# Batch 1's attention inside a fused attention and MoE kernel: shared query rows and one burst of transposes

## The chip, the cores and the metric

The kernel runs on one core of one Trainium2 chip. The metric is device time in microseconds of one execution, taken as the median of several runs. In the text, TensorE is the matmul engine (PE in the profile; PEld are its weight loads), VectorE is DVE, ScalarE is ACT, GpSimd is POOL, and SP is the engine whose queue issues the output DMAs.

## The reference

For 8 batches of 8 heads, 576 tokens and 64 channels a head, two attentions are computed and added. One is local: each query sees the keys at a distance under 4. The other is pooled: queries, keys and values are averaged over groups of 4 tokens, 144 queries attend to 144 keys, and each result is repeated for its 4 tokens. The sum, as 4608 rows of 512 channels, goes through a feed-forward layer.

```
out_d = sm_attn(q_d, k_d, v_d)            # means over groups of 4 tokens
out_up = np.repeat(out_d, factor, axis=2)
scores = np.where(mask, scores, -1e9)     # |i - j| < 4
out_local = np.matmul(attn, v)
x = (out_up + out_local) as [B * S, H * D]
h = x @ w_in;  g = h / (1 + exp(-1.702 h));  out = g @ w_out
```

## The kernel before

**Order of the work.** The order on every engine is the order in which the program's text issues instructions; nothing is rescheduled. The feed-forward layer (the MoE matmuls) runs over 9 groups of 512 tokens. For group g, `mm1` (L732) multiplies x by w_in into 16 blocks of 128 hidden channels, 4 matmuls of 128x512 each, and ScalarE applies the sigmoid product to each block (L728). `mm2` (L749) multiplies by w_out, 16 matmuls into each of four token tiles of 128 tokens (L781), and ScalarE evicts each tile (L766) before it is stored. While group g runs, the attention of batch g + 1 is put between these matmuls: `attention` (L666 to L714) returns a list of pieces, and a list of positions says before which step each piece goes. Steps 0 to 15 are the hidden blocks of `mm1`, step 16 + n is matmul n of `mm2`. Group 0 has its own list, `POS_0` (L811), and batch 1 is the batch that it carries. Other batches go by `POS` (L810); batch 0 is written out by hand ahead of the loop.

**PSUM.** There are three double tiles PA[0] to PA[2], each of two banks, and two single ones, PM[0] and PM[1] (in the profile all are pa and pm). The MoE matmuls use PM in turn, and in group 0 also PA[0]: token tiles 0 and 1 accumulate in PM, tiles 2 and 3 in the two banks of PA[0], in the order of eight matmuls at a time, tiles 0 and 1 first and tiles 2 and 3 from matmul 16. Attention's scores take all three double tiles. Batch 1's other pieces use PA[1] and PA[2] only (`slots`, the pair of heads taken modulo 2). Group 1 begins with two blocks at once, one in PM and one in PA[1].

**A batch's attention.** Heads go in pairs (`hp`, 0 to 3), two pairs at a time as far as the scores:

- Scores of two pairs (`scores_mixed`, L365 and L377): 80 matmuls of a 32-row, 64-column tile for five chunks of local keys and 24 for the pooled keys. ScalarE takes the exponentials (L415, L421), and VectorE zeroes what lies outside the band (L429).
- `av` (L446, L468): 20 matmuls with the local weights and 20 with the pooled ones, each a tile of 64 rows and 64 columns, so that four of them lie in the array. A 65th column of ones gives the sums for the softmax. In each matmul the 64 output partitions are queries of one head; the two heads of a pair stand in different halves of the partitions.
- `normalise` (L484, L485): VectorE takes the reciprocals of the sums and multiplies, from PSUM to `y` in bf16.
- `transp` (L499, L509): 26 matmuls with the identity, again tiles of 64 rows and 64 columns, turn `y` into channels by tokens, as fp32 in a double tile. Each handles one head.
- `copy_od` (L623): ScalarE copies the 144 pooled results, each four times, to `od` in SBUF, in two instructions. `od` has two buffers.
- `merge` (L644, L650): VectorE adds the local results and `od` and writes the pair's rows of `xT`, which `mm1` of the next group reads.

Batch 1's pieces and steps before the change: scores of pairs 0 and 1 at 16, their exponentials at 18, the second scores with exponentials at 30, values and normalisation of pairs 0 and 1 at 46, transposes and merge of pair 0 at 52 and of pair 1 at 56, values of pairs 2 and 3 at 65, transposes and merge of pair 2 at 71 and of pair 3 at 75. Step 79 is the last matmul of group 0. At step 41 a further piece computes the pooled values on TensorE (L334).

Of the kernel before, what the change touches and what calls it, by code (L numbers as in the profile page):

```python
# [8 lines left out]
FP32 = mybir.dt.float32  # L9
BF16 = mybir.dt.bfloat16  # L10
AF = mybir.ActivationFunctionType
ALU = mybir.AluOpType
# [7 lines left out]
def kernel(  # L20
# [9 lines left out]
    nc = tc.nc  # L30
    B, H, S, D = q.shape
    SD = S // 4
    HP = H // 2
# [16 lines left out]
    work = ctx.enter_context(tc.tile_pool(name="work", bufs=2))  # L50
# [9 lines left out]
    xT = [persist.tile([128, B * S], BF16, name=f"xT{i}") for i in range(HP)]  # L60
    vbs = [persist.tile([128, 5, H, 65], BF16, name=f"vb{i}") for i in range(2)]
    vds = [persist.tile([128, 3, HP, 65], BF16, name=f"vd{i}") for i in range(2)]
    es = [persist.tile([128, 2, 304], BF16, name=f"es{i}") for i in range(4)]
    eds = [persist.tile([128, 2, 480], BF16, name=f"ed{i}") for i in range(2)]
# [7 lines left out]
    def ps_tile(n=None):  # L72
        if n is None:
            n = turn["a"] % 3
            turn["a"] += 1
        return PA[n]

    def pm_tile():
        turn["m"] += 1
        return PM[turn["m"] % 2]  # L80
# [60 lines left out]
    def ident(pos, n, c0, c1):  # L141
        return id128[64 * pos : 64 * pos + n, 64 * pos + c0 : 64 * pos + c1]
# [277 lines left out]
    def exp_down(qd, sd):  # L420
        nc.scalar.activation(  # L421
            out=eds[qd][:, :, 0:432], in_=sd[:, :, 0:432],
            func=AF.Exp, scale=inv_sqrt_d / 16.0,
        )
# [66 lines left out]
    def transp(y, n=None):  # L491
# [23 lines left out]
                )  # L515
        return x

    def av_local0(hp, o, chunks):
        E, vb = es[hp], vbs[0]
        for i in chunks:  # L520
            for j in range(2):
                for par in range(2):
                    pos, c0 = i % 2, 65 * (i // 2 * 2 + j)
                    nc.tensor.matmul(  # L524
                        o[64 * pos : 64 * pos + 64, par, c0 : c0 + 65],
                        lhsT=E[64 * par : 64 * par + 64, j, 60 * i : 60 * i + 64],
                        rhs=vb[64 * par : 64 * par + 64, i, 2 * hp + j, :],
                        start=True, stop=True,
                        tile_position=(64 * par, 64 * pos),
                    )  # L530
# [98 lines left out]
    def sub(t, off, *dims):  # L629
        return bass.AP(  # L630
            tensor=t.tensor, offset=t.offset + off,
            ap=[list(t.ap[0])] + [list(d) for d in dims],
        )
# [22 lines left out]

    def warm(n, cols=512, t=None, z=wz):
        t = pm_tile() if t is None else t  # L660
        for _ in range(n):
            nc.tensor.matmul(
                t[:, 0:cols], lhsT=z[:, 0:128], rhs=z[:, 0:cols], start=True, stop=True
            )

    def attention(b, slots=None):  # L666
        st = {}

        def s_pe(qd):
            st["s", qd], st["d", qd] = scores_mixed(b, qd)  # L670

        def s_act(qd):
            if qd == 0:
                nc.scalar.preload_act_table_set("exp_and_others")
            exp_local(qd, st["s", qd])
            exp_down(qd, st["d", qd])
            if qd == 1:
                nc.scalar.preload_act_table_set("silu_and_others")
            mask_local(qd)

        def s1():
            s_pe(1)
            s_act(1)

        def avn(*hps):
            def f():
                for hp in hps:
                    st["o", hp] = av(b, hp, slots and slots[hp % 2])
                for hp in hps:
                    st["y", hp] = normalise(st["o", hp])  # L690
            return f

        def tr(*hps):
            def f():
                for hp in hps:
                    st["x", hp] = transp(st["y", hp], slots and slots[hp % 2])
                for hp in hps:
                    od = copy_od(st["x", hp])
                    merge(b, hp, st["x", hp], od)
            return f  # L700

        first = [lambda: s_pe(0), lambda: s_act(0), s1, avn(0, 1)]
        if b == 1:
            return first + [tr(0), tr(1), avn(2, 3), tr(2), tr(3)]

        def av_tr():
            for hp in (2, 3):
                st["o", hp] = av(b, hp)
            st["x", 0] = transp(st["y", 0])
            for hp in (2, 3):  # L710
                st["y", hp] = normalise(st["o", hp])
            merge(b, 0, st["x", 0], copy_od(st["x", 0]))

        return first + [av_tr, tr(1, 2, 3)]  # L714

    def hps_mm(g, ffc, dmc, acc):
        nc.tensor.matmul(  # L717
# [90 lines left out]
            f()  # L808

    POS = [13, 16, 35, 45, 56, 69]  # L810
    POS_0 = [16, 18, 30, 46, 52, 56, 65, 71, 75]  # L811
    VDP_0 = 41

    o, y, x = {}, {}, {}
# [89 lines left out]
    for g in range(n_groups):  # L904
        b = g + 1
# [33 lines left out]
        if b < B:  # L939
            for n, f in zip(POS if g else POS_0, attention(b, None if g else (1, 2))):  # L940
                steps.setdefault(n, []).append(f)
# [37 lines left out]
```

## Time and profile before

| | before |
|---|---|
| runs, us | 320.72, 318.91, 321.6; median 320.72 |
| profiled execution, us | 320.13 |
| its span, us | 318.4 |
| mean granted TensorE clock | 0.995 |
| TensorE busy, matmuls | 301.9 us, 95% |
| ScalarE, GpSimd, VectorE busy | 58%, 44%, 41% |
| DMA | 40.02 MB, mean 126 GB/s |

The profile shows one execution. The span runs from the first instruction to the last; the profiled execution's own time is 1.7 us more. A group's row names line, engine, operation, what is written and read, and how often; a row of a timeline gives start, length, and in brackets how long the engine stood idle before and what ended that. The chain of waits follows the execution back from its last instruction, at each step to what released it. "issue" is time in which an engine waited for nothing that the profile shows. Matmuls overlap in the array: a MoE matmul's row is 379 ns long, but the next one starts 216 ns behind it. Some matmul records can be missing from a trace.

### The profile page before, as it was taken

The numbers are of one execution on the slowest core, as the hardware profiler recorded it, in microseconds if no ns is written. First come the engines' busy times: TensorE is split into PE (matmuls) and PEld (weight loads), VectorE is DVE, ScalarE is ACT, GpSimd is POOL, SyncE is SP. The second block draws the span as 40 slices with busy tenths as digits, with TensorE's granted clock in tenths as the row PEclk, the third lists the DMA queues.
The fourth block names the chain that finished last, engine by engine and source line by source line (L and its number), as shares of the span: only waits on it lengthen the run. The fifth ranks groups of instructions, "written<-read, shape, count | busy, mean of one in ns | idle before, by whom it ended". The sixth has DMA issues, their size and how long they took to land.

```text
span 318.4 us, 10941 instructions
## 1 busy us (share of the span) xinstructions
PE 301.9 (95%) x4872; PEld 156.5 (49%) x4923; DVE 130.3 (41%) x219; ACT 184.9 (58%) x320; POOL 138.7 (44%) x170
## 2 busy tenths in 40 slices
PE   7699999999899999999999999999999999999995
PEld 4465454545454555445545454445445544444444
DVE  5855625831575047704780288017811650000000
ACT  5445782567546684659465846584667556415611
POOL 8773790099227940695059604980294000000000
PEclk9979999999999999999999999999999999999999
DMA  7999999999949923995299619961810210020011
GB/s 120 118 200 209 182 126 213 166 229 227 165 128 203 207 64 103 190 209 101 72 197 205 128 48 213 206 136 39 176 41 3 70 68 2 0 99 33 2 65 67
DMA packets 64078, 40.02 MB, mean 126 GB/s; under 512 B 44064, under 2 KB 55456, under 8 KB 64032
## 3 DMA queue, kind: packets, MB, share of 16 engines
q1 hardware_dynamic: 44496, 24.32, 37.3%
q0 software_dynamic: 19392, 14.95, 33.8%
q8 instruction: 38, 0.62, 0.9%
q14 instruction: 8, 0.07, 0.1%
q10 hardware_dynamic: 144, 0.07, 0.1%
HBM read 44.83 MB, written 9.44 MB: 170 GB/s over the span
## 4 chain that ended last, share of the span: by engine, by line
PE 91%; issue 3%; DMA 2%; DVE 1%; POOL 1%; ACT 1%; POOLq 0%
PE pm L781 35%; PE pm L717 35%; PE pa L717 4%; PE pa L365 2%; PE pa L377 2%; DMA qb<-in_q_dram 2%; PE pa L781 2%; PE pa L446 2%; PE pa L499 2%; PE pa L468 2%; PE pm L796 1%; PE pm L334 1%; PE pa L509 0%; PE pa L524 0%; DVE qT L267 0%
## 5 line engine op out<-in xcount | busy, mean ns | idle before, releaser
L717 PE MATMUL pm<-xT,w_in_bf 128*128 128x512 bf16 x495 | 118.2, 379 | 1.2 <-ACT xT L616 0.2
L781 PE MATMUL pm<-w_out_bf,gT 128*128 128x512 bf16 x499 | 114.4, 379 | 4.2 <-issue 4.1
L728 ACT ACTIVATE gT<-pm 128x512 bf16<-128x512 f32 x128 | 76.3, 598 | 43.7 <-PE pm L717 43.7
L717 PEld LDWEIGHTS <-w_in_bf 128*128 128x128 bf16 x576 | 55.7, 98 | 66.5 <-issue 0.5
L781 PEld LDWEIGHTS <-gT 128*128 128x128 bf16 x560 | 52.1, 98 | 60.1 <-issue 0.8
L429 DVE TENSOR_TENSOR es<-es,mask 128x600 bf16<-128x600 bf16 x28 | 17.6, 643 | 94.6 <-ACT es L415 93.8
L297 POOL TENSOR_TENSOR pq<-kT 128x576 f32<-128x576 bf16 x13 | 15.1, 1165 | 70.5 <-DVE kT L267 70.5
L766 ACT ACTIVATE osb<-pm 128x512 f32<-128x512 f32 (+2 forms) x35 | 20.5, 586 | 38.2 <-PE pm L781 30.3
L623 ACT COPY od<-pa 128x384 f32<-128x384 f32 (+1 forms) x56 | 19.0, 407 | 27.2 <-PE pa L509 20.7
L485 DVE TENSOR_TENSOR y<-pa,rc 128x896 bf16<-128x896 f32 x28 | 30.6, 1092 | 1.0
L415 ACT ACTIVATE es<-pa 128x600 bf16<-128x600 f32 x32 | 19.7, 668 | 9.5 <-PE pa L365 9.4
L644 DVE TENSOR_TENSOR xT<-pa,od 128x570 bf16<-128x570 f32 x28 | 21.0, 752 | 8.8 <-ACT od L623 8.8
L313 POOL TENSOR_TENSOR v<-v 112x512 f32<-112x512 f32 x18 | 23.0, 1279 | 0.0
L768 DVE TENSOR_SCALAR osb<-pm 128x128 f32<-128x128 f32 x1 | 0.3, 291 | 55.0 <-ACT osb L766 55.0
L267 DVE STREAM_TRANSPOSE kT<-kb 128x576 f32<-128x576 f32 x16 | 20.0, 1250 | 4.3 <-DMA kb<-in_k_dram 4.2
L267 DVE STREAM_TRANSPOSE qT<-qb 128x576 f32<-128x576 f32 x16 | 19.9, 1242 | 0.6 <-POOL kdT L301 0.2
L717 PE MATMUL pa<-xT,w_in_bf 128*128 128x512 bf16 x64 | 20.0, 379 | 0.0
L307 POOL CAST vb<-vf 128x2560 bf16<-128x2560 f32 x6 | 13.9, 2319 | 13.7 <-DMA vf<-in_v_dram 11.3
L365 PEld LDWEIGHTS <-kT 32*64 32x64 bf16 x1280 | 14.2, 104 | 7.7 <-issue 4.9
L365 PE MATMUL pa<-qT,kT 32*64 32x60 bf16 x1280 | 16.4, 198 | 1.3 <-DVE qT L267 1.3
L221 POOL DMA_DIRECT2D vb<-in_v_dram x20 | 13.7, 698 | 9.1 <-DMA w_in_bf<-in_moe_w_in_dram 4.0
L297 POOL TENSOR_TENSOR pq<-qT 128x576 f32<-128x576 bf16 x14 | 16.0, 1145 | 0.1
(90 smaller groups left out, 274.2 us busy)
## 6 DMA issues: line engine op xcount, KB each, us to landing
out_dram<-osb SPq DMA_DIRECT2D x35, 256.0 KB, 2.1
vf<-in_v_dram SPq DMA_DIRECT2D x60, 128.0 KB, 6.8
v<-in_v_dram SPq DMA_DIRECT2D x36, 192.0 KB, 5.5
kb<-in_k_dram POOLq DMA_DIRECT2D x16, 288.0 KB, 7.2
qb<-in_q_dram POOLq DMA_DIRECT2D x16, 288.0 KB, 8.6
w_in_bf<-in_moe_w_in_dram POOLq DMA_DIRECT2D x4, 512.0 KB, 7.2
w_out_bf<-in_moe_w_out_dram POOLq DMA_DIRECT2D x4, 512.0 KB, 12.9
vb<-in_v_dram POOLq DMA_DIRECT2D x20, 64.0 KB, 6.4
```

The lines of the kernel that those rows point to most:

```text
L267: nc.vector.transpose(out=t32.rearrange("p (i c) -> p c i", c=18), in_=store[b, qd].bitcast(FP32).rearrange("p (c d) -> p c d", c=18),)
L297: nc.gpsimd.tensor_tensor(out=t1, in0=sv[:, :, 0:2, :], in1=sv[:, :, 2:4, :], op=ALU.add)
L313: eng.tensor_tensor(out=t1[0:112], in0=x[:, :, 0:2, :], in1=x[:, :, 2:4, :], op=ALU.add)
L365: nc.tensor.matmul(sp[r // 2][64 * par : 64 * par + 64, r % 2, 60 * i : 60 * i + 60], lhsT=kT[b, qd][rows, k0 : k0 + 64, a], rhs=qT[b, qd] ...
L415: nc.scalar.activation(out=es[2 * qd + u][:, :, 0:300], in_=sp[u][:, :, 0:300], func=AF.Exp, scale=inv_sqrt_d,)
L485: nc.vector.tensor_tensor(out=y[:, xs], in0=ov[:, :, :, 0:D], in1=rc[:, xs].to_broadcast([128, n, 7, D]), op=ALU.mult,)
L623: nc.scalar.copy(out=od[:, 4 * t0 : 4 * (t0 + n)].rearrange("p (t f) -> p t f", f=4), in_=x[:, xx, 288 : 288 + n, None].to_broadcast([128, ...
L644: eng.tensor_tensor(out=sub(xT[hp], t0 + 3, (57, 2), (114, 5), (1, 57)), in0=sub(x, 3, (509, 2), (57, 5), (1, 57)), in1=sub(od, 3, (57, 2) ...
L717: nc.tensor.matmul(acc, lhsT=w_in_bf[:, dmc, ffc * 128 : (ffc + 1) * 128], rhs=xT[dmc][:, g * TG : g * TG + TG], start=(dmc == 0), stop=(d ...
L728: nc.scalar.activation(out=gT[:, ffc, :], in_=acc, func=AF.Silu, scale=GELU_SCALE)
L766: eng.activation(out=osb, in_=ap, func=AF.Copy, scale=1.0 / GELU_SCALE)
L781: nc.tensor.matmul(ops[t], lhsT=gT[:, ffc, t * 128 : (t + 1) * 128], rhs=w_out_bf[:, ffc, :], start=(ffc == 0), stop=(ffc == n_ffc - 1),)
```

## The change

Only batch 1's attention is changed, and of that the pieces behind the scores, and the list of steps.

- `av_rows` puts both heads of a pair on the same partitions. A matmul is still a tile of 64 by 64, and there are still 40 for a pair, in another order: chunk i of the queries goes to the lower or upper 64 partitions by i's parity, and the heads stand beside each other in columns.
- `normalise_rows` has the same two VectorE instructions, and then a copy of 64x64 on ScalarE that brings one head's block beside the other's.
- `transp_rows` takes 60 or 64 rows and both heads' 128 columns at once: 13 matmuls for a pair instead of 26, tiles of 64 rows and 128 columns, in transpose mode, with bf16 output. The outputs of two pairs share a double tile (`x_pair`: 0 and 2 in PA[1], 1 and 3 in PA[2]).
- `copy_od_rows` copies the pooled results four times each, as 256 and 320 columns; `merge_rows` adds in three instructions, of 456, 117 and 3 columns.
- The pieces are now: scores at 16, exponentials at 18, second scores at 29, values of pairs 0 and 1 at 46, values of pairs 2 and 3 at 54, and at 65 the transposes of all four pairs in one burst, followed by their copies and merges.

```diff
@@ -515,6 +515,78 @@
                 )
         return x
 
+    def av_rows(b, hp, n=None):
+        o = ps_tile(n)
+        E, Ed, vb, vd, u = es[hp], eds[hp // 2], vbs[b % 2], vds[b % 2], hp % 2
+
+        def local(i, par, j):
+            pos, c0 = i % 2, 65 * (i // 2 * 2 + j + par)
+            nc.tensor.matmul(
+                o[64 * pos : 64 * pos + 64, par, c0 : c0 + 65],
+                lhsT=E[64 * par : 64 * par + 64, j, 60 * i : 60 * i + 64],
+                rhs=vb[64 * par : 64 * par + 64, i, 2 * hp + j, :],
+                start=True, stop=True,
+                tile_position=(64 * par, 64 * pos),
+            )
+
+        def down(kc, j, pos, slot, q0, last=2):
+            nc.tensor.matmul(
+                o[64 * pos : 64 * pos + 64, j, 65 * slot : 65 * slot + 65],
+                lhsT=Ed[64 * j : 64 * j + 48, u, SD * kc + q0 : SD * kc + q0 + 64],
+                rhs=vd[64 * j : 64 * j + 48, kc, hp, :],
+                start=(kc == 0), stop=(kc == last),
+                tile_position=(64 * j, 64 * pos),
+            )
+
+        for i in (0, 2):
+            for j in range(2):
+                for par, e in ((0, 0), (1, 1), (1, 0), (0, 1)):
+                    local(i + e, par, j)
+        left = [(local, (4, par, j)) for j in range(2) for par in range(2)]
+        left += [(down, (kc, j, 0, 6 - 6 * j, 0)) for kc in range(3) for j in range(2)]
+        right = [(down, (0, j, 1, 5 + j, 64, 0)) for j in (1, 0)]
+        right += [(down, (kc, j, 1, 6 - 6 * j, 64)) for kc in range(3) for j in (1, 0)]
+        right += [(down, (kc, j, 1, 4 + j, 128)) for kc in range(3) for j in (1, 0)]
+        for n in range(len(right)):
+            for side in (left, right):
+                if n < len(side):
+                    side[n][0](*side[n][1])
+        return o
+
+    def normalise_rows(o):
+        y = work.tile([128, 14, D], BF16, name="y", tag="y", bufs=4)
+        rc = work.tile([128, 2, 7, 1], FP32, name="rc", tag="rc")
+        ov = o[:, :, 0:455].rearrange("p x (c e) -> p x c e", e=65)
+        nc.vector.reciprocal(rc, ov[:, :, :, 64:65])
+        nc.vector.tensor_tensor(
+            out=y.rearrange("p (x c) d -> p x c d", x=2),
+            in0=ov[:, :, :, 0:D], in1=rc.to_broadcast([128, 2, 7, D]), op=ALU.mult,
+        )
+        nc.scalar.copy(out=y[64:128, 5, :], in_=y[64:128, 12, :])
+        return y
+
+    def x_pair(n=None):
+        t = ps_tile(n).rearrange("p x n -> p (x n)").bitcast(BF16)
+        t = t.rearrange("p (x n) -> p x n", x=2)
+        return [t[:, :, 512 * u : 512 * u + 512] for u in range(2)]
+
+    def transp_rows(y, x):
+        def put(pos, c0, n, src):
+            nc.tensor.matmul(
+                x[:, pos, c0 : c0 + n], lhsT=src, rhs=ident(pos, src.shape[0], 0, n),
+                is_transpose=True, start=True, stop=True, tile_position=(64 * pos, 0),
+            )
+
+        for m in range(3):
+            for par in range(2):
+                for pos in range(2 if m < 2 else 1):
+                    c0 = 8 * par + 2 * m
+                    put(pos, 120 * m + 60 * par, 60, y[64 * pos : 64 * pos + 60, c0 : c0 + 2, :])
+                if m == 2:
+                    c0 = 6 - 2 * par
+                    put(1, 240 + 64 * par, 64, y[64:128, c0 : c0 + 2, :])
+        put(0, 360, 64, y[0:64, 6:8, :])
+
     def av_local0(hp, o, chunks):
         E, vb = es[hp], vbs[0]
         for i in chunks:
@@ -656,6 +728,28 @@
 
 
 
+    def copy_od_rows(x):
+        od = work.tile([128, S], FP32, name="od", tag="od")
+        for xx, c0, t0, n in ((0, 360, 0, 64), (1, 240, 64, 80)):
+            nc.scalar.copy(
+                out=od[:, 4 * t0 : 4 * (t0 + n)].rearrange("p (t f) -> p t f", f=4),
+                in_=x[:, xx, c0 : c0 + n, None].to_broadcast([128, n, 4]),
+            )
+        return od
+
+    def merge_rows(b, hp, x, od):
+        t0 = b * S
+        row = x.ap[1][0]
+        for at, col, dims, from_x in (
+            (3, 3, ((228, 2), (114, 2), (1, 114)), ((120, 2), (row, 2), (1, 114))),
+            (459, 243, ((1, 117),), ((1, 117),)),
+            (0, 0, ((1, 3),), ((1, 3),)),
+        ):
+            nc.vector.tensor_tensor(
+                out=sub(xT[hp], t0 + at, *dims), in0=sub(x, col, *from_x),
+                in1=sub(od, at, *dims), op=ALU.add,
+            )
+
     def warm(n, cols=512, t=None, z=wz):
         t = pm_tile() if t is None else t
         for _ in range(n):
@@ -699,9 +793,25 @@
                     merge(b, hp, st["x", hp], od)
             return f
 
-        first = [lambda: s_pe(0), lambda: s_act(0), s1, avn(0, 1)]
-        if b == 1:
-            return first + [tr(0), tr(1), avn(2, 3), tr(2), tr(3)]
+        def avn_rows(*hps):
+            def f():
+                for hp in hps:
+                    st["o", hp] = av_rows(b, hp, slots[hp % 2])
+                for hp in hps:
+                    st["y", hp] = normalise_rows(st["o", hp])
+            return f
+
+        def tr_rows():
+            for u in range(2):
+                st["x", u], st["x", u + 2] = x_pair(slots[u])
+            for hp in range(HP):
+                transp_rows(st["y", hp], st["x", hp])
+            for hp in range(HP):
+                merge_rows(b, hp, st["x", hp], copy_od_rows(st["x", hp]))
+
+        scores_first = [lambda: s_pe(0), lambda: s_act(0), s1]
+        if slots:
+            return scores_first + [avn_rows(0, 1), avn_rows(2, 3), tr_rows]
 
         def av_tr():
             for hp in (2, 3):
@@ -711,7 +821,7 @@
                 st["y", hp] = normalise(st["o", hp])
             merge(b, 0, st["x", 0], copy_od(st["x", 0]))
 
-        return first + [av_tr, tr(1, 2, 3)]
+        return scores_first + [avn(0, 1), av_tr, tr(1, 2, 3)]
 
     def hps_mm(g, ffc, dmc, acc):
         nc.tensor.matmul(
@@ -808,7 +918,7 @@
             f()
 
     POS = [13, 16, 35, 45, 56, 69]
-    POS_0 = [16, 18, 30, 46, 52, 56, 65, 71, 75]
+    POS_0 = [16, 18, 29, 46, 54, 65]
     VDP_0 = 41
 
     o, y, x = {}, {}, {}

```

## The prediction

> **What bounds the kernel now.** I read the page first, then the chain of waits from 40 to 62 us, the stretch in which batch 1's attention lies, then the timelines of TensorE, ScalarE and VectorE there, and last the groups by shape.
>
> ```profile
> PE 301.9 (95%) x4872; PEld 156.5 (49%) x4923; DVE 130.3 (41%) x219; ACT 184.9 (58%) x320; POOL 138.7 (44%) x170
> ...
> q8 instruction: 38, 0.62, 0.9%
> ...
> PE 91%; issue 3%; DMA 2%; DVE 1%; POOL 1%; ACT 1%; POOLq 0%
> ```
>
> TensorE is the bound almost from end to end: 95% busy, 91% of the chain. Whatever shortens its own queue is worth its full time; work on the others costs only where TensorE waits. So I look for the places where TensorE does not start the next matmul in time. Start time, length and piece in the chain:
>
> ```profile
> 44.47 0.66 ACT es L415
> ...
> 45.17 2.10 PE pa L781 x9
> ...
> 51.89 0.37 issue
> 52.27 0.21 PE pa L509 x3
> ...
> 53.78 0.16 issue
> 53.94 1.67 PE pa L781 x7
> 55.61 0.22 PE pm L781
> ...
> 58.05 0.14 issue
> 58.19 0.35 PE pa L499 x20
> ```
>
> Three kinds of holes: at 45.17 a MoE matmul into PA[0] waits for the exponential that reads PA[0]; at 51.89 and 58.05 TensorE stands inside or before a transpose burst with nothing to wait for; and 0.16 us of "issue" follows each burst. The last kind is no wait. The timeline of TensorE, matmuls and then weight loads:
>
> ```profile
> 52.41 1.04 PE L781 MATMUL pm<-w_out_bf,gT 128*128 128x512 bf16 x4
> 53.38 0.35 PE L499 MATMUL pa<-id,y 60*64 60x60 bf16 x20
> 53.56 0.22 PE L509 MATMUL pa<-id,y 48*64 48x48 bf16 x6
> 53.94 1.67 PE L781 MATMUL pa<-w_out_bf,gT 128*128 128x512 bf16 x7 [0.16 <-issue]
> 55.45 0.38 PE L781 MATMUL pm<-w_out_bf,gT 128*128 128x512 bf16 x1
> ...
> 60.91 0.38 PE L717 MATMUL pm<-xT,w_in_bf 128*128 128x512 bf16 x1
> ```
> ```profile
> 53.71 0.55 PEld L781 LDWEIGHTS <-gT 128*128 128x128 bf16 x4
> ```
>
> Between this burst (step 56) and the next (step 65) the program has nine matmuls; the rows show 7 + 1, and the weights of a first one are loaded at 53.71, 0.23 us before the first recorded one. One record is missing and its matmul sits in the "issue". So a transpose burst costs from 53.07 (52.41 plus three steps of 0.216 and a slow first one) to 53.71, less the normal step: 0.64 - 0.22 = 0.42 us. Of that 26 x 8.2 ns = 0.21 is streaming, 0.09 getting in and 0.12 getting out.
>
> ```profile
> 57.24 0.81 PE L781 MATMUL pm<-w_out_bf,gT 128*128 128x512 bf16 x3
> ```
>
> The two real holes are 0.56 us (0.37 idle plus the 0.19 that the last matmul still ran) before 52.27, and 0.21 before 58.19: the third of this row starts at 57.67, and a burst otherwise begins 0.31 behind (53.38 - 53.07). They have one thing in common with the later ones:
>
> ```profile
> 84.51 0.28 PE L468 MATMUL pa<-vd,ed 48*64 48x65 bf16 x9 [0.88 <-issue]
> 88.51 0.21 PE L446 MATMUL pa<-vb,es 64*64 64x65 bf16 x1 [0.19 <-issue]
> 220.57 0.22 PE L499 MATMUL pa<-id,y 60*64 60x57 bf16 x4 [0.17 <-issue]
> ```
>
> Counted in the program's list of TensorE instructions they stand at 1726, 1982, 2750, 3006 and 7870 (one more, 0.32 us, at 7614, time 216.57, too short to show as a row of its own): all 190 past a multiple of 256. The page's instruction queue moved 38 packets, 0.62 MB, for 9,795 recorded instructions: 63 B each, so a packet carries 256. I read these holes as waits for the next block of instructions, where a block is eaten in under some 5 us because it is full of small matmuls. They are 0.56 + 0.21 in batch 1 and 1.07 + 0.38 + 0.32 + 0.36 = 2.1 us later, again with 0.19 added to each row's idle time.
>
> **The change part by part.** The sum is made against the profiled execution, 320.13 us, of which 318.4 is the span; the three runs' median, 320.72, is 0.6 above it.
>
> Second scores at step 29 instead of 30. The chain above: three matmuls instead of two then lie between these scores and the first one into PA[0]. Scores and exponential both move 0.22 us earlier, and the hole at 45.17 shrinks by as much. Scores of pooled keys go into PA[2], which the first pair's exponential still reads:
>
> ```profile
> 42.34 0.90 ACT L421 ACTIVATE ed<-pa 128x864 bf16<-128x864 f32 x1
> ```
> ```profile
> 43.55 0.27 PE L377 MATMUL pa<-qdT,kdT 32*64 32x144 bf16 x4
> ```
>
> It ends at 43.24; they now come at 43.55 - 0.22 = 43.33, so the cover holds by 0.1. **-0.22** (0 if it is missed).
>
> Transposes. Removed: 4 bursts of 26, 4 x 0.42 = 1.70 us. Added: one of 52, each half the array high and all of it wide. No transpose-mode matmul is in this trace; the nearest shape is L547:
>
> ```profile
> 20.66 0.27 PE L547 MATMUL pa<-vd,ed 48*128 48x65 bf16 x6
> ```
> ```profile
> 20.65 0.15 PEld L547 LDWEIGHTS <-ed 48*128 48x128 bf16 x6
> ```
> ```profile
> L547 PE MATMUL pa<-vd,ed 48*128 48x65 bf16 x24 | 1.1, 194 | 0.0
> ...
> L781 PE MATMUL pm<-w_out_bf,gT 128*128 128x512 bf16 x499 | 114.4, 379 | 4.2 <-issue 4.1
> ```
>
> (0.27 - 0.19) / 5 = 16 ns from one to the next, the two halves alternating as in the new code. 52 x 16 = 0.83, with in and out 1.04: **-0.65**. Low end 8.2 ns as now (-1.07); high end no overlap of loads, whose row has 0.15 us for six of some 95 ns, so 52 x 0.095 = 4.9 (+3.5). I take 16, from the row of the same tile shape.
>
> The Trainium skill, TensorE: Matmul & The Clock Gate, section LDWEIGHTS, speaks against this part: a load takes columns / 1.2 ns, whatever its rows, so twice the columns cost what half the loads save. By its 107 ns, two halves side by side, the burst would be an estimated 52 x 53 ns = 2.8 us and the whole change 1.1 us slower than before. L547's row disagrees: 16 ns.
>
> Attention-times-value bursts. 40 matmuls a pair as now, the same columns, four of them left on half the tiles: +0.05. Both bursts go before all transposes, so the second (step 54) needs PA[1] and PA[2] from VectorE:
>
> ```profile
> 49.88 0.24 DVE L484 RECIPROCAL rc<-pa 128x14 f32<-128x14 f32 x1 [3.69 <-PE pa L468]
> 50.16 1.09 DVE L485 TENSOR_TENSOR y<-pa,rc 128x896 bf16<-128x896 f32 x1
> ...
> 51.43 1.09 DVE L485 TENSOR_TENSOR y<-pa,rc 128x896 bf16<-128x896 f32 x1
> 53.25 0.76 DVE L644 TENSOR_TENSOR xT<-pa,od 128x570 bf16<-128x570 f32 x1 [0.73 <-ACT od L623]
> 54.04 0.17 DVE L650 TENSOR_TENSOR xT<-pa,od 128x6 bf16<-128x6 f32 x1
> ```
>
> All moved by 0.22: PA[1] is free at 51.03, PA[2] at 52.30. The first burst is left at 49.90 and eight matmuls (1.73) end at 51.73; PA[2] is wanted at 52.2. Instruction 1726 now falls 21 matmuls into this burst, at 51.9; its block, which came at 52.27, comes then or 0.2 sooner. Together 0.3 us of waiting here, in place of the 0.56 in the transposes. Instruction 1982 now falls seven MoE matmuls behind the transpose burst, at 57.7, some 5.7 us after 1726 where 5.9 were needed (52.27 to 58.19); what is left of its 0.21 goes into the wait at the end of the stretch. **-0.77 + 0.3 = -0.47** (bounds: -0.77 when the block comes in time, +0.6 when both holes stay and another opens). TensorE then stands at 52.85; eleven matmuls (2.37) later, the burst.
>
> Behind the burst. It runs 55.3 to 56.15, and 15 MoE matmuls (3.24) bring TensorE to group 1 at 59.45. Its first matmul overwrites the PSUM tile of token tile 0, whose eviction is now queued on ScalarE behind eight copies of od; with two od buffers, copies 3 and 4 wait for merges 1 and 2.
>
> ```profile
> 53.84 0.70 ACT L623 COPY od<-pa 128x384 f32<-128x384 f32 x2 [0.61 <-PE pa L509]
> 57.44 0.60 ACT L766 ACTIVATE osb<-pm 128x512 f32<-128x512 f32 x1 [2.90 <-PE pm L781]
> ```
>
> Outputs 0 and 2 share PA[1], so the first copy waits for 39 transposes: 56.1. A copy pair keeps its 576 columns, 0.70: 56.8. A merge is now 456 + 117 + 3 columns; with L644's 570 in 0.75 and L650's 6 in 0.17, 1 ns a column and some 0.16 fixed: 0.63 + 0.28 + 0.17, overlapping by 0.08: 0.9, step 0.83. Merges 1 and 2 end 57.75 and 58.6, copy pair 4 runs 58.65 to 59.35, the eviction ends 59.9. Group 1 starts at 59.95, a wait of **+0.45** (0 to +0.9). Merges 3 and 4 end at 59.5 and 60.3, before TensorE wants PA[1] (second matmul, 60.15) and their rows (fifth and seventh, 60.8 and 61.2). The four 64x64 copies on ScalarE, 0.25 each, lie in its idle time (2.90 us before 57.44).
>
> Sum: -0.22 - 0.65 + 0.05 - 0.47 + 0.45 = **-0.85**. No DMA, and nothing on SP's and GpSimd's queues, changes place; TensorE waits for no landing in this stretch now and reaches none more than 0.5 us sooner.
>
> Later batches. 104 instructions fewer shift every later block border against the bursts. Blocks made of bursts and some 20 loads or matmuls of the MoE stay about as many, so I take 0; bounds -2.1 (all later holes close) and +2 (as much opens).
>
> **The rivals.**
> - The block borders fall well: -0.85 - 2.1 gives 317.8. For: the holes hang on position. Against: half of the comparable blocks have no hole now, so little is to be had beyond it.
> - The borders fall badly: +2, 321.9.
> - The chain behind the burst is longer (od buffers, a late merge): from +0.45 to +1.4, 320.8. For: it has no slack, and VectorE and ScalarE alternate in it.
> - Slower: the wide transposes do not overlap their loads as L547 does. At 95 ns, two halves side by side: 52 x 48 ns = 2.5 us instead of 0.83, +1.7, 321.5; one after another: 4.9, +4.1, 324.0. The change breaks even at (0.83 + 0.85) / 52 = 32 ns each. Against it: L547. The page's load rule, above, is the first of the two.
> - Slower: TensorE's clock drops in the burst. It has dropped once:
>
> ```profile
> 16.00:24.00 8.00, 7.72 (x191) 5.30 (x192) 4.64 (x13) 3.83 (x7) 5.97 (x10) 0.79 1.23 200
> ...
> 49.00:61.00 12.00, 10.85 (x297) 5.94 (x300) 8.21 (x15) 3.92 (x11) 0.18 (x1) 1.00 1.08 198
> ```
>
> At 0.79 (the last column but two) the burst and the 15 matmuls behind it, 4.1 us, take 1.1 us more: 321.0; at half speed 4.1 more: 324.0. Now the clock is 1.00 through four bursts. The Trainium skill's page TensorE: Matmul & The Clock Gate, PE-mode transpose, says that such transposes do not count as busy; no run here shows it, and one microsecond is little.
>
> **How the numbers follow.** 320.72 - 0.85 = 319.87, so 319.8 for the likeliest case, with 318.8 to 320.7 as its own range. Chances: forecast 0.58, good borders 0.14, bad borders 0.06, longer chain 0.11, transposes half overlapped 0.04, serial 0.04, clock 0.03. The runs themselves lie 2.7 us apart, and 1%, 3.2 us, is about what a measurement of this kernel can tell from no change. Low end 317.7 takes in the good borders, high end 321.9 the longer chain, the half overlapped transposes and the bad borders; the serial transposes are outside. Faster by over 1% needs good borders and a better batch 1: 0.11. Slower by over 1%: serial transposes, most of the clock, and a bad draw of borders on top of another loss: 0.09. Within 1%: 0.80.
>
> **What would show it.** In the profile after: the wait for the exponential at 45 shorter by 0.2; one burst of 52 transposes in 0.8 to 0.9 us with granted clock 1.00; no issue hole in it; the hole inside the second value burst at 0.1 to 0.4; ScalarE's eviction of the first output tile ending near 59.9 with group 1's first matmul right behind it, near 60, against 60.91 now. Wrong would be: transposes over 32 ns each, group 1 starting after 60.9, or issue holes beyond 80 us that sum to less than 0.5 or more than 3.5.

## The result, and the profile after

| | before | after |
|---|---|---|
| median, us | 320.23 (22 runs, 318.45 to 323.11) | 318.44 (22 runs, 317.18 to 323.02) |
| ratio, 95% interval | | 0.9944, 0.9924 to 0.9965 |
| profiled execution, us (span) | 320.13 (318.4) | 317.25 (315.4) |
| mean granted TensorE clock | 0.995 | 0.994 |

The change makes the kernel 1.8 us faster, by the interval 1.1 to 2.4. All ratios here are taken over fast runs, without those more than 1.5% above the fastest run of the same kernel (323.02 here, for instance, and later the profiled run with 104 instructions ahead). The page of the kernel after:

```profile
PE 300.0 (95%) x4821; PEld 155.4 (49%) x4871; DVE 129.2 (41%) x223; ACT 185.6 (59%) x324; POOL 138.8 (44%) x170
...
q8 instruction: 38, 0.62, 0.8%
...
PE 89%; issue 3%; DMA 2%; DVE 2%; ACT 1%; POOL 1%; POOLq 0%; ACTq 0%
```

TensorE is the bound as before, and the instruction queue again moved 38 packets. To find where the time came from, I cut the span at the first scores of batch 1 (step 16 of group 0) and of batch 2 (the same step of group 1); everything the change touches lies between them. The timelines of TensorE, first of the kernel before, then of the one after:

```profile
39.20 0.28 PE L365 MATMUL pa<-qT,kT 32*64 32x60 bf16 x20
...
72.23 0.33 PE L365 MATMUL pa<-qT,kT 32*64 32x60 bf16 x32
```
```profile
38.96 0.32 PE L365 MATMUL pa<-qT,kT 32*64 32x60 bf16 x30
...
70.95 0.33 PE L365 MATMUL pa<-qT,kT 32*64 32x60 bf16 x32
```

This stretch fell from 33.03 to 31.99 us: 1.04 us. What stands inside it, TensorE's timeline of the kernel after:

```profile
44.71 2.10 PE L891 MATMUL pa<-w_out_bf,gT 128*128 128x512 bf16 x9
...
51.51 0.34 PE L524 MATMUL pa<-vb,es 64*64 64x65 bf16 x17
...
52.13 0.33 PE L524 MATMUL pa<-vb,es 64*64 64x65 bf16 x17
...
54.77 0.38 PE L891 MATMUL pm<-w_out_bf,gT 128*128 128x512 bf16 x1
55.09 0.96 PE L575 MATMUL pa<-id,y 60*128 60x60 bf16 x52
56.21 1.61 PE L891 MATMUL pm<-w_out_bf,gT 128*128 128x512 bf16 x6 [0.16 <-issue]
57.66 1.89 PE L891 MATMUL pa<-w_out_bf,gT 128*128 128x512 bf16 x8
59.64 0.38 PE L827 MATMUL pm<-xT,w_in_bf 128*128 128x512 bf16 x1
```

The wait for the exponential is gone (44.71 follows the matmuls before it without one). The transposes are one burst of 52. Group 1 begins at 59.64, 20.68 us behind the first scores, where it was 60.91 and 21.71. The second value burst has a gap in its middle: its second pair starts 0.62 us behind the first, where a run below has 0.40. VectorE's and ScalarE's timelines say what ended that gap, and what group 1 waited for:

```profile
50.98 1.09 DVE L561 TENSOR_TENSOR y<-pa,rc 128x896 bf16<-128x896 f32 x1
...
56.62 3.39 DVE L748 TENSOR_TENSOR xT<-pa,od 128x456 bf16<-128x456 bf16 x12 [1.88 <-ACT od L734]
```
```profile
55.89 1.31 ACT L734 CAST od<-pa 128x256 f32<-128x256 bf16 x4 [0.87 <-PE pa L575]
57.60 1.49 ACT L734 CAST od<-pa 128x256 f32<-128x256 bf16 x4 [0.40 <-DVE xT L748]
58.98 1.10 ACT L876 ACTIVATE osb<-pm 128x512 f32<-128x512 f32 x2
```

Pair 1's normalisation, which must leave PA[2], ends at 52.07. The first eviction starts at 58.98 behind all eight copies of `od`, of which the last four had to wait for a merge (0.40); at 0.60 us, as before, it ends at 59.58, and group 1 starts at 59.64.

### The profile page after: what moved, and what is told of

It reads as the page before. It is cut to its first block, busy times and chain, and to the rows that moved or that the text cites. A ratio compares the mean times of both kernels' runs of the same rounds, so it can differ in the third digit from the quotient of the medians.

```text
span 315.4 us, 10842 instructions
## 1 busy us (share of the span) xinstructions
PE 300.0 (95%) x4821; PEld 155.4 (49%) x4871; DVE 129.2 (41%) x223; ACT 185.6 (59%) x324; POOL 138.8 (44%) x170
## 4 chain that ended last, share of the span: by engine, by line
PE 89%; issue 3%; DMA 2%; DVE 2%; ACT 1%; POOL 1%; POOLq 0%; ACTq 0%
PE pm L827 35%; PE pm L891 35%; PE pa L827 4%; PE pa L365 2%; DMA qb<-in_q_dram 2%; PE pa L377 2%; PE pa L446 2%; PE pa L499 2%; PE pa L891 2%; PE pa L468 1%; PE pm L906 1%; PE pm L334 0%; PE pm L756 0%; ACT od L734 0%; DVE qT L267 0%
## 5 line engine op out<-in xcount | busy, mean ns | idle before, releaser
L838 ACT ACTIVATE gT<-pm 128x512 bf16<-128x512 f32 x128 | 76.3, 598 | 43.5 <-PE pm L827 43.5
L429 DVE TENSOR_TENSOR es<-es,mask 128x600 bf16<-128x600 bf16 x28 | 16.8, 612 | 94.2 <-ACT es L415 93.4
L297 POOL TENSOR_TENSOR pq<-kT 128x576 f32<-128x576 bf16 x13 | 15.1, 1165 | 67.3 <-DVE kT L267 57.5
L695 ACT COPY od<-pa 128x384 f32<-128x384 f32 (+1 forms) x48 | 16.2, 407 | 21.6 <-PE pa L509 18.7
L485 DVE TENSOR_TENSOR y<-pa,rc 128x896 bf16<-128x896 f32 x24 | 26.2, 1091 | 0.8
L716 DVE TENSOR_TENSOR xT<-pa,od 128x570 bf16<-128x570 f32 x24 | 18.0, 751 | 6.2 <-ACT od L695 6.2
```

What stands on the lines that cost most here:

```text
L297: nc.gpsimd.tensor_tensor(out=t1, in0=sv[:, :, 0:2, :], in1=sv[:, :, 2:4, :], op=ALU.add)
L429: nc.vector.tensor_tensor(out=ev, in0=ev, in1=mask, op=ALU.mult)
L485: nc.vector.tensor_tensor(out=y[:, xs], in0=ov[:, :, :, 0:D], in1=rc[:, xs].to_broadcast([128, n, 7, D]), op=ALU.mult,)
L716: eng.tensor_tensor(out=sub(xT[hp], t0 + 3, (57, 2), (114, 5), (1, 57)), in0=sub(x, 3, (509, 2), (57, 5), (1, 57)), in1=sub(od, 3, (57, 2) ...
L838: nc.scalar.activation(out=gT[:, ffc, :], in_=acc, func=AF.Silu, scale=GELU_SCALE)
```

## The experiments

Each is read by the length of the stretch above. Behind it the traces are alike: from the first scores of batch 7 to the end 80.13 to 80.15 us in all twelve profiles, and from one batch's first scores to the next 32.74 to 32.76 us where no hole lies between. What is over five times 32.75 in batches 2 to 6 is therefore loss, and stands in the last column; the holes at block borders (below) are in the column before it.

| kernel | first scores at, us | stretch, us | border holes in it, us | loss in batches 2 to 6, us |
|---|---|---|---|---|
| before | 39.20 | 33.03 | 0.77 | 2.24 |
| before, again | 38.88 | 33.26 | 1.00 | 1.06 |
| second scores sooner, alone | 38.44 | 32.91 | 0.87 | 1.37 |
| after | 38.96 | 31.99 | 0.16 | 0.59 |
| after, again | 38.76 | 31.99 | 0.37 | 1.62 |
| after, third | 38.23 | 32.19 | 0.61 | 4.57 |
| after, second scores late | 38.02 | 32.21 | 0 | 2.16 |
| after, narrow transposes | 41.05 | 33.70 | 1.60 | 1.91 |
| after, 104 instructions ahead | 43.53 | 32.51 | 0.52 | 2.78 |
| after, eviction first | 41.77 | 31.59 | 0 | 2.02 |
| after, both waits | 40.72 | 31.37 | 0 | 1.26 |
| after, two bursts | 39.72 | 34.27 | 0 | 2.24 |

The part ahead of the first scores, which only the run with 104 instructions edits, took 38.0 to 41.8 us in the others: times of single executions say little about an effect of 0.2 us, the stretch does. The length of that part goes with the granted clock in it. Where the clock stayed at 1.00 (four profiles) it took 38.0 to 38.8 us, with one spell of 3.4 us at 0.50 (five) 38.9 to 41.1, and with 6.8 us at 0.50 (three, the one with 104 instructions among them) 40.7 to 43.5.

**Both kernels again.** No edit: the changed kernel once more, later a third profile of it, and the kernel before against itself.

> The changed kernel once more, as a control. Border theory (holes in TensorE's queue are waits for a block of 256 instructions): about 1.8 us faster than before; from batch 1's first scores to batch 2's first scores 32.0 us within 0.2, holes later than that under 1 us together and, where there are any, at the same instructions (190 past a multiple of 256). Chance theory (the later holes fall anywhere, the first profile was a lucky one): holes at other instructions, or as many as before, 2 us.

> The kernel before, unchanged, once more against itself. Theory (the stretch of batch 1 gives 1.04 us of the 1.8 that the times show, and the rest is what waits for instruction blocks add up to in one execution or another): the ratio is 1.000 within 0.003; the stretch is between 32.8 and 33.4 us with holes of 0.6 to 1.0 us in all at the instructions 1726 and 1982, and the later holes stand again at instructions 190 past a multiple of 256, but with other lengths, 1.0 to 2.5 us in all. Rival (the kernel before always loses 2.1 us there, and the change closes most of it): again 2.1 us in the same four places.

> The changed kernel, unchanged, a third time, for its profile. Theory: the stretch is 32.0 us within 0.3; later holes at instruction 2750 and 6334 (second to last batches), 0.4 to 2.0 us in all, as in its other two profiles. Rival (the change closes the later holes): under 0.4 us in all.

The changed kernel gave 0.9947 (0.9915 to 0.9980), the kernel before against itself 1.0003 (0.9971 to 1.0034). Mean stretch: (33.03 + 33.26) / 2 = 33.15 before, (31.99 + 31.99 + 32.19) / 3 = 32.06 after, so the change is worth 1.09 us there. The later holes change their length from one execution to the next: the 1.62 us of the repeat exceed the 1 us expected of it, the 4.57 us of the third profile the 0.4 to 2.0 (1.6 of them are not hole but clock, see the last section). The change does not close them. The rival, that the kernel before always loses 2.1 us there, falls with its 1.06.

The two last profiles hold a record of every matmul (4923 and 4871). In them no "issue" of 0.16 us follows a burst, and the costs of bursts can be read without correction. TensorE's timeline of the third profile of the kernel after:

```profile
54.05 0.38 PE L891 MATMUL pm<-w_out_bf,gT 128*128 128x512 bf16 x1
54.36 0.96 PE L575 MATMUL pa<-id,y 60*128 60x60 bf16 x52
55.25 1.47 PE L891 MATMUL pm<-w_out_bf,gT 128*128 128x512 bf16 x6
57.17 0.38 PE L891 MATMUL pm<-w_out_bf,gT 128*128 128x512 bf16 x1 [0.45 <-issue]
```

From the MoE matmul ahead of the burst to the one behind it 1.205 us (1.20 by the rounded rows), less the normal step of 0.216: the burst costs 0.99. The hole before 57.17 is a block border: six steps from 55.25 end at 56.55, so 0.62 us (0.61 unrounded). The same border in the second profile of the kernel before, TensorE's matmuls and then its weight loads:

```profile
56.36 0.81 PE L781 MATMUL pm<-w_out_bf,gT 128*128 128x512 bf16 x3
58.10 0.35 PE L499 MATMUL pa<-id,y 60*64 60x60 bf16 x20 [0.93 <-DVE y L485]
```
```profile
57.10 0.10 PEld L499 LDWEIGHTS <-y 60*64 60x64 bf16 x1 [0.42 <-DVE rc L484]
58.10 0.21 PEld L499 LDWEIGHTS <-y 60*64 60x64 bf16 x16 [0.90 <-issue]
```

This pair teaches how far to trust a releaser. The first row names VectorE's `y`. But the load that reads `y`, instruction 1981 of TensorE's list, had run at 57.10, and the matmul that belongs to it, number 1982, came 1.00 us later. Nothing of the data can stand between the two: the `y` named is that of pair 3, which pair 2's transposes do not read, and in the first profile of this kernel the same matmul started at 58.19, before that `y` was done (57.89 + 1.09 = 58.98). 1982 is 190 past a multiple of 256, as 1726 is.

What it did wait for stands in the DMA records. The instruction queue's 38 packets have 16,384 bytes each. Between 38 and 260 us the twelve profiles have 34 holes in which TensorE stood idle for over 0.12 us without a true releaser (the 0.16 us of missing records left out). Every one ends 1.26 to 1.79 us behind the end of a packet of this queue, and always of the packet that belongs to the border: the sixth at 1726, the seventh at 1982, the tenth at 2750. The waits with a true releaser end between 1.0 and 6.0 us behind the last packet.

**Second scores sooner, alone.** The kernel before, with one number changed.

```diff
-    POS_0 = [16, 18, 30, 46, 52, 56, 65, 71, 75]
+    POS_0 = [16, 18, 29, 46, 52, 56, 65, 71, 75]
```

> The kernel before with one edit: its second scores at step 29 instead of 30, everything else as it was. Theory (each part of the change is worth what it takes out of TensorE's queue): the wait of 0.21 us at 45.17 closes, so the stretch from batch 1's first scores to group 1's is 33.03 - 0.21 = 32.8 us and the time 0.2 us shorter (ratio 0.9993, too little for the times to show). Rival (the whole gain hangs on the earlier scores, since they move the exponential and all behind it): the stretch comes near the 31.99 of the kernel after. Second rival (the cover of 0.1 us is missed): the scores of pooled keys wait for PA[2], the stretch stays at 33.0.

From the first scores to the second 3.90 us instead of 4.11: 0.21 gained. The border at 1726 has no hole this time and the one at 1982 has 0.87, where the two had 0.56 and 0.21. Without border holes the stretch is 32.91 - 0.87 = 32.04, against 33.03 - 0.77 = 32.26 and 33.26 - 1.00 = 32.26 in the two profiles of the kernel before: 0.22 less, as expected. The ratio is 0.9969 (0.9943 to 0.9996), whose near end is 0.13 us.

**Second scores late.** The same the other way round: the kernel after, with these scores back at step 30.

```diff
-    POS_0 = [16, 18, 29, 46, 54, 65]
+    POS_0 = [16, 18, 30, 46, 54, 65]
```

> The changed kernel with the second scores at step 30 again. If the wait for the exponential is what this step saves: the wait before the first matmul into PA[0] comes back and the stage from batch 1's first scores to batch 2's is 0.22 longer than in the changed kernel, 32.2. If the wait at the end of the stage sets its length anyway (rival): the same 32.0, since that wait shrinks by as much.

The stretch is 32.21, 0.22 more than 31.99, and the wait is back; TensorE's timeline:

```profile
43.98 1.02 PE L891 MATMUL pa<-w_out_bf,gT 128*128 128x512 bf16 x4 [0.26 <-ACT es L415]
```

Ratio 0.9968 (0.9936 to 1.0001). This part is settled from both sides.

**Narrow transposes.** The kernel after, each transpose cut in two tiles of 64 by 64, all 104 in the one burst and still in transpose mode.

```diff
+            for h in range(2):
                 nc.tensor.matmul(
-                x[:, pos, c0 : c0 + n], lhsT=src, ...
+                    x[64 * h : 64 * h + 64, pos, c0 : c0 + n], lhsT=src[:, h, :], ...
-                is_transpose=True, start=True, stop=True, tile_position=(64 * pos, 0),
+                    is_transpose=True, start=True, stop=True,
+                    tile_position=(64 * pos, 64 * h),
```

> The changed kernel with each transpose cut into two of 64 rows and 64 columns, 104 instead of 52, still in one burst and in transpose mode. If streaming is what counts and the gain is only three entries and exits fewer: the burst still streams in 0.85 to 0.95 us, the stage is 32.0 to 32.2. If the wide tile itself is the gain (rival): 104 times 15 ns, 1.56 us, stage 32.6 or more. The instruction count is that of the kernel before again, so by the border theory later holes may come back: up to 1 us more than in the changed kernel; by the chance theory no difference there.

Ratio 1.0021 (0.9991 to 1.0050): slower than the kernel after. The stretch of 33.70 us misses the 32.0 to 32.2 of the theory, though without its hole the burst streams in 0.92 us, as the theory asked. The burst in TensorE's timeline:

```profile
57.17 0.69 PE L576 MATMUL pa<-id,y 60*64 60x60 bf16 x58
59.28 0.57 PE L576 MATMUL pa<-id,y 60*64 60x60 bf16 x46 [1.42 <-issue]
```

One tile follows another by (0.69 - 0.19) / 57 = 8.8 ns, where a wide one takes (0.96 - 0.19) / 51 = 15.1: two narrow ones cost 17.6 ns against 15.1, 0.13 us over the burst. Of the 1.71 us by which the stretch grew, 1.60 are one hole, 59.28 less 57.17 + 58 x 0.0088, and it lies at instruction 1982 again, which in this longer list falls into the burst. In this execution the 52 additional matmuls cost more by the border that they brought into the burst than by the time that they run.

**104 instructions ahead.** The kernel after, with 52 more small matmuls on zeros in the warm-up ahead of everything, so that every later block border lies where it did before the change.

```diff
     warm(21, 336)
+    warm(52, 32)
```

> The changed kernel with 52 tiny matmuls (104 instructions) more among the warm-up matmuls, which add nothing to the result and run while TensorE waits for the first loads. All block borders of the batches after 1 then stand where they stood before the change. Border theory: 0.3 to 1.0 us slower than the changed kernel, with holes in batch 2's value bursts at the same places as in the profile before. Chance theory, or the gain lying in batch 1 alone: as fast as the changed kernel within 0.3.

Ratio 1.0026 (0.9990 to 1.0062). The time does not settle it: the first scores came at 43.53, and among the other profiles, without these matmuls, the start already differs by 3.8 us. The places do. In batch 2 the hole moved from the first value burst to the second, counted from that batch's first scores from 12.71 us in the repeat of the kernel after (11.99 in its first profile) to 16.14; TensorE's timeline, of the repeat of the kernel after and then of this one:

```profile
83.46 0.26 PE L468 MATMUL pa<-vd,ed 48*64 48x65 bf16 x6 [0.86 <-issue]
```
```profile
92.18 0.21 PE L446 MATMUL pa<-vb,es 64*64 64x65 bf16 x1 [1.02 <-issue]
```

Counted in each kernel's own list, the first is at 2750 and the second at 3006. All holes of 0.15 us or more in batches 2 to 6 of the twelve profiles stand at eight places: 2750, 3006, 4030, 4286, 5310, 6334, 7614 and 7870, each 190 past a multiple of 256. (Counted by the weight loads in the traces, two instructions to a load, the last six come out two to four lower. The traces also show one semaphore instruction of TensorE in each batch; with these counted, apart from those ahead of the first matmul, all eight stand 192 or 193 past.) The lists with 104 more instructions use 3006, 4030, 4286, 7614 and 7870; the shorter ones 5310 and 6334; both 2750. Which borders hurt is decided by what lies around them.

**Eviction first.** The kernel after, with the copies and merges of pairs 2 and 3 as a piece of their own at step 68, so that ScalarE evicts the first output tile ahead of them.

```diff
-            for hp in range(HP):
+            for hp in range(2):
                 merge_rows(b, hp, st["x", hp], copy_od_rows(st["x", hp]))
+        def end_rows():
+            for hp in range(2, HP):
+                merge_rows(b, hp, st["x", hp], copy_od_rows(st["x", hp]))
...
-    POS_0 = [16, 18, 29, 46, 54, 65]
+    POS_0 = [16, 18, 29, 46, 54, 65, 68]
```

> The kernel after with one edit: the od copies and merges of pairs 2 and 3 are issued at step 68 instead of right behind those of pairs 0 and 1, so that the eviction of output tile 0 goes ahead of od copies 3 and 4 on ScalarE. Theory (the 0.25 us in which TensorE stands before group 1 is the eviction queued behind the copies, which wait for merges): that wait goes and the stretch is 31.99 - 0.25 = 31.75 us. Rival (the wait is the rest of the instruction block's hole, or comes back at once because merges 3 and 4 are now late for group 1's fifth and seventh matmul): the stretch stays at 32.0 or grows to 32.4, with a hole inside group 1's first eight matmuls.

The stretch is 31.59, 0.40 less; 0.25 was expected. TensorE's timeline:

```profile
59.02 1.46 PE L895 MATMUL pm<-w_out_bf,gT 128*128 128x512 bf16 x6 [0.16 <-issue]
60.31 1.89 PE L895 MATMUL pa<-w_out_bf,gT 128*128 128x512 bf16 x8
62.04 0.38 PE L831 MATMUL pm<-xT,w_in_bf 128*128 128x512 bf16 x1
```

60.31 + 8 x 0.216 = 62.04: group 1 waits for nothing, and its first eight matmuls follow in steps of 0.216. The miss is instructive. I had counted the 0.16 us at the border in the kernel after as a loss of its own. But group 1 starts when the eviction ends, so a hole ahead of it only shortens the wait: 0.16 + 0.25 = 0.41 is the chain's price whatever lies in it. The other profiles fit. In the repeat of the kernel after the hole was 0.37 and the wait 0.05, with the stretch of 31.99 unchanged; with the second scores late there was no hole and the wait was 0.42; in the third profile 0.61 of border hole took the place of the whole 0.41, and the stretch grew by 0.20.

**Both waits.** In addition, the second value burst a step later.

```diff
-    POS_0 = [16, 18, 29, 46, 54, 65, 68]
+    POS_0 = [16, 18, 29, 46, 55, 65, 68]
```

> As the run with the eviction first, and the second value burst at step 55 instead of 54. Theory (the 0.19 us in the middle of that burst is the wait for pair 1's normalisation, not an instruction block): one more MoE matmul ahead of the burst covers it, the stretch is 31.99 - 0.25 - 0.19 = 31.55 us and the time 0.45 us under the kernel after, ratio 0.993 to before if nothing else moves. Rival (it is the block that ends at this place of the list): the 0.19 us stays wherever the burst stands, 31.75.

The stretch is 31.37, another 0.22 less, and the burst has no gap: its second pair starts 0.40 us behind the first instead of 0.62. TensorE's timeline:

```profile
53.49 0.34 PE L524 MATMUL pa<-vb,es 64*64 64x65 bf16 x17
...
53.89 0.33 PE L524 MATMUL pa<-vb,es 64*64 64x65 bf16 x17
```

So that gap was the wait for pair 1's normalisation. By the stretch this version beats the kernel after by 0.6 us; the times do not show it (0.9942, 0.9914 to 0.9969).

**Two bursts.** The kernel after, with its transposes in two bursts of 26.

```diff
-            return scores_first + [avn_rows(0, 1), avn_rows(2, 3), tr_rows]
+            return scores_first + [avn_rows(0, 1), tr_rows(0, 1),
+                                   avn_rows(2, 3), tr_rows(2, 3)]
...
-    POS_0 = [16, 18, 29, 46, 54, 65]
+    POS_0 = [16, 18, 29, 46, 55, 63, 73]
```

> The kernel after with its 52 transposes in two bursts of 26 (pairs 0 and 1 at step 55, the second value burst at step 63, pairs 2 and 3 at step 73), tiles and mode unchanged. Theory (a burst costs 0.21 us to get in and out, besides 15 ns for each transpose; the rest of the gain is the shape of the tiles and the waits): +0.21 for the second way in and out, -0.19 for the wait for pair 1's normalisation, -0.25 for the eviction, +0.15 for pair 3's normalisation, one step short: 31.9 us, between 31.6 and 32.3. Rival (it is the single burst that pays, by more than its way in and out): at least 32.6.

34.27 us: a miss, and on the rival's side, which asked for at least 32.6. Ratio 1.0023 (0.9994 to 1.0052). TensorE's timeline has three waits, all with their releaser named:

```profile
52.89 0.55 PE L575 MATMUL pa<-id,y 60*128 60x60 bf16 x26 [0.33 <-DVE y L561]
...
56.81 0.34 PE L524 MATMUL pa<-vb,es 64*64 64x65 bf16 x17 [1.06 <-DVE xT L748]
...
63.97 2.32 PE L828 MATMUL pm<-xT,w_in_bf 128*128 128x512 bf16 x9 [0.94 <-DVE xT L748]
```

Against the starts that would be due without them they cost 0.40 + 1.22 + 1.10 = 2.72 us (the last: 63.97 less 62.65, the matmul before it, less a step of 0.216), and 34.27 - 2.72 = 31.55. A burst costs what the theory said: the second, from its neighbours' steps, 0.59, two of them 0.20 more than one of 0.99. That closes the account: the run with both waits removed, 31.37, plus 0.20 is 31.57. What I missed are the chains: both merges of a pair of pairs must leave PSUM before the next values, and the last ones come too late for group 1. The single burst's own way in and out is worth 0.2; that the work behind it runs once and in the shadow of 15 MoE matmuls is worth ten times that here.

## Why the prediction was right, point by point

It said 319.8, in a range of 317.7 to 321.9. The sum behind it, -0.85 (as printed its terms add up to -0.84), was made against the profiled execution, 320.13, but taken off 320.72, the median of three runs; off the 320.23 of 22 runs it gives 319.4. Measured were 318.44 and a gain of 1.8 (1.1 to 2.4), about twice the forecast, which lies outside that interval. That the time fell into a range of 4.2 us says little; what can be checked is the stretch, which gave 1.09, and its terms.

| term of the sum | predicted, us | measured, us | from |
|---|---|---|---|
| second scores sooner | -0.22 | -0.21 and -0.22 | scores alone; scores late |
| four bursts to one | -0.65 (1.70 to 1.04) | -0.71 (1.70 to 0.99) | the two complete profiles |
| value bursts | +0.05 | +0.07 | the two complete profiles |
| holes in the stretch | -0.47 | -0.55 and -0.78 | 0.77 and 1.00 to the 0.22 of the wait for pair 1 |
| wait before group 1 | +0.45 | +0.41 | eviction first |
| block borders in later batches | 0 | none that stands out | mean loss 1.87 over five profiles with the longer list, 2.07 over seven with the shorter |

With -0.21 for the first term, the five terms of the stretch add up to -0.99 or -1.22, for the two values of the holes; the stretch gave -1.09.

- *Transposes.* 16 ns from the neighbouring shape became 15.1. Both rivals of transposes that do not overlap their loads fall: the break-even was 32 ns. The rule in the Trainium skill, TensorE: Matmul & The Clock Gate, section LDWEIGHTS, that a load takes time by its columns, does not price this burst: the estimate from it was 53 ns a transpose. Nor do the recorded loads go by columns: in the third profile those of 128 columns (`y`, L575) took 93 ns on average, those of 64 columns (L499) 106.
- *The clock in the burst.* The windows of the kernel after show 1.00 (the last column but two):

```profile
49.00:61.00 12.00, 11.36 (x250) 6.15 (x246) 9.52 (x21) 5.58 (x16) 0.18 (x2) 1.00 1.14 198
```

- *The second value burst.* Predicted were 0.3 us, most of them for a border at 1726; it is 0.22, all of it the wait for PA[2], which the prediction named as well. At this border the changed kernel had no hole longer than that wait in any of its three profiles.
- *The wait before group 1.* Mechanism and size hold. The prediction let the remains of the hole at 1982 go into this wait, and that is what they do, as long as they stay under 0.41.
- *The mis-sized term.* It is the holes: "-0.77 + 0.3 = -0.47". The kernel before loses 0.8 to 1.0 us at its two borders in this stretch, of which I knew one sample; the changed one loses nothing there that the chain does not cover, apart from 0.2 in one profile. The mark that the prediction set for the holes beyond 80 us, 0.5 to 3.5 in sum, held in the three profiles of the changed kernel: 0.59, 1.62 and, without the 1.6 of the clock, 2.9.
- *What stays open.* The times fell by 1.8, the stretch by 1.09. 0.7 us have no place in the traces: the later batches lose as much with either list, and the tail is equal. The interval reaches down to 1.1, so it may be chance. The granted clock is one part of that chance, since it differs between executions: among runs of about the same clock, the medians of the repeat lie 1.2 to 1.3 us under those of the kernel before (319.40 to 318.08 at 1.000, 320.14 to 318.99 at 0.995, 321.93 to 320.71 at 0.989), close to the stretch. For the 22 runs of the kernel before that stand in the result the clock is not on record. Also open is why a block is late in one execution and not in the next. In the third profile the packet behind border 2750 started 10.85 us after batch 2's first scores and took 1.39 us, in the first 9.58 and 1.08: it is fetched later, and no run here tells why.

## What to carry to other kernels

Cut the span at events that both kernels have, and compare the stretch: it settled 0.2 us where the times settled 1. Before you price a hole, ask what it waits for and what lies behind it: a hole ahead of a wait that a chain sets anyway is free, and a wait for instructions can carry the name of an innocent engine. Where an engine runs many small instructions, count them and see where the borders of their blocks fall: the run with narrow transposes suggests, in one execution, that two merged into one of the same total time can still pay.

## What the runs showed of the hardware

A hole can cost more than its length. In the third profile of the kernel after, the border at 2750 held TensorE for 2.0 us, and then the clock fell; TensorE's timeline, and the windows with the granted clock in the last column but two:

```profile
81.98 0.45 PE L468 MATMUL pa<-vd,ed 48*64 48x65 bf16 x14
84.24 0.26 PE L468 MATMUL pa<-vd,ed 48*64 48x65 bf16 x6 [1.82 <-issue]
84.44 4.18 PE L891 MATMUL pm<-w_out_bf,gT 128*128 128x512 bf16 x11
```
```profile
82.00:84.00 2.00, 0.42 (x32) 0.28 (x17) 1.34 (x2) 0.65 (x1) 0.00 (x0) 1.00 0.94 156
84.00:85.00 1.00, 0.76 (x8) 0.43 (x9) 0.42 (x2) 0.00 (x0) 0.00 (x0) 0.68 0.75 159
85.00:86.00 1.00, 1.00 (x4) 0.30 (x2) 0.92 (x1) 0.01 (x1) 0.00 (x0) 0.50 1.01 303
86.00:87.00 1.00, 1.00 (x4) 0.33 (x3) 0.00 (x0) 0.58 (x1) 0.20 (x1) 0.50 0.24 84
87.00:88.00 1.00, 1.00 (x4) 0.38 (x3) 0.00 (x0) 0.00 (x0) 1.00 (x1) 0.61 0.56 209
```

Eleven MoE matmuls took 4.18 us, where ten steps of 0.216 and one of 0.38 make 2.54: 1.6 us on top of the 2.0, and a loss of 4.57 in this execution. The hole of 1.6 us in the run with narrow transposes left the clock at 1.00. The Trainium skill, TensorE: Matmul & The Clock Gate, section Why this matters for your kernels, says to allow no idle gaps over about 3 us; here the clock fell behind one of 2.0. Length alone does not decide: in the start TensorE stood idle for 2.09 us in two profiles, and the clock fell to 0.50 within 0.5 us in one (kernel before, idle until 16.19) and stayed at 1.00 in the other (second scores late, idle until 15.65). What else decides, no run here tells.
